# FFT mixing and a gated feed-forward layer on one Trainium2 core: the first batch with one spectrum tile per unit, filters copied across partitions, rotated inverse tables and units by halves of d

## The chip, the core and the metric

The kernel runs on one core of a Trainium2 chip. The core has a matrix engine (TensorE, PE), a vector engine (VectorE, DVE), a scalar engine (ScalarE, ACT), a general engine (GpSimd, POOL) and a queue engine (SyncE, SP). They run side by side, each in its own program order, and wait for each other by semaphores. Sixteen DMA engines move data between the chip's memory and the core's on-chip memory of 128 partitions; SP's DMAs (hardware queue q1) and POOL's (software queue q0) share them. PE writes to PSUM, which DVE and ACT can read and POOL can't. The metric is the device time of one execution in microseconds (us); lower is better.

## The reference

Two stages follow each other; only these lines matter:

```python
def _attn_ref(x, filt_r, filt_i):          # x: 8 x 3008 x 256, filters: 1505 x 256
    X = np.fft.rfft(x, axis=1)
    Y = X * (filt_r + 1j * filt_i)[None, :, :]
    return np.fft.irfft(Y, n=x.shape[1], axis=1).astype(np.float32)

def _moe_ref(x, w_in, w_out, beta):        # x: 24064 x 256, 256 -> 2048 -> 256
    h = x @ w_in
    g = h * (1.0 / (1.0 + np.exp(-beta * h)))
    return (g @ w_out).astype(np.float32)
```

The first stage, run on each of 8 batches along the sequence, filters every column in the frequency domain; the second is a feed-forward layer on all 24,064 rows.

## The kernel before

**The transform as matmuls.** 3008 = 47 x 64. A transform goes in two stages forward (s1 with table t1 over the 47, s2 with tables t2 over the 64, which hold the twiddle factors), a product with the filters, and two stages back (s3 with tables t3, the transposes of t2; s4 with t4, the transpose of t1). Partitions 0 to 63 of a spectrum tile hold real parts, 64 to 127 imaginary parts; the 24 values of k1 (NK) index the tiles. A complex product needs both `real * filt_r - imag * filt_i` and `imag * filt_r + real * filt_i`, so it crosses the two halves of the partitions.

**Main loop.** `NSTEP` = 47 blocks of 512 rows x 16 column blocks of the hidden layer. Step s does two matmuls with w_in (L722, `hps`), one Silu on ACT (L731, `gT`), then whatever the plan puts at this step, then, two steps late, four matmuls with w_out (L742, `acc`). `plan` and `at(step, ...)` are a timetable written out by hand: the transforms of batches 1 to 7 (s1 L557, s2 L573 with the products L587 to L592, s3 L602, s4 L631) are spread over the steps of the batch before. Between s1 and s2, and between s3 and s4, data goes through scratch memory (`d1`, `d2`): stores and loads are SP DMAs, whose queue is in program order. POOL adds the two halves of a product (`yh`, L592), loads x (`load_x`, L332 and L333, a cast from float32 to bf16 in the DMA) and scales w_out by 1/beta (`scale_wout`, L345).

**The setup, batch 0.** Its transform can't hide under anything and runs before the loop, in an order written out by hand. It generates the tables from iotas with Sin on ACT (`t2_part`: two more column sets with another sign, `dup`: copies that put the column blocks side by side in `tw_sb`), loads batch 0 (`x0`, eight DMAs on POOL's queue) and the filters (`load_filters`, L94: half on SP, half on POOL; `seen`, a tiny DMA on SP, holds SP's back until the third quarter of x0 has landed). `s1_0` is stage 1, `a0_turn` transposes its result. Then come six units (8 values of k1 x 128 columns of d): `s2_0` twice per unit, once with the ordinary columns of t2 and once with the halves swapped, each followed by one product on DVE with `ff_sb`, which holds filt_r in partitions 0 to 63 and filt_i in 64 to 127 (L407, L405); `s3_0` sums both products with two sets of inverse tables, `t3c`, made by `t3_part` (transposes, evacuated on ACT). `z_turn` and `s4_0` are the last stage and write y, which the main loop reads; every y write must be there before its first step. Between them stand `s1_early`, the first eight of sixteen stage-1 matmuls of batch 1, and `turn_t4`, which makes t4 (transpose, ACT copy, a POOL multiply of its first rows).

The loop's plan for batch 1 has the other eight stage-1 units in its first six steps, `turn_t3` (L614: t3 from t2, at steps 6, 9, 12), the loads of a2 at step 8 (L565), s2 from step 15, s3 five steps later; at step 4, `copy_fr` (L537, L538: POOL copies filt_r from `ff_sb` to both halves of `fr_sb`, which the products of the loop need, six copies); `load_wout` and `scale_wout` for the third and fourth quarter of w_out at steps 2 and 3. x of batch 2 is loaded at steps 10, 13, 16 and 19.

Evacuations of PSUM go through `evac` (L115 on ACT, L117 and L119 on DVE), so many operations share these lines and are told apart by tile names. `spsum` (three buffers of two banks) and `tpsum` (two) rotate.

Of the kernel before, what the change touches and what calls it, by code (L numbers as in the profile page):

```python
# [10 lines left out]
P = 128  # L11
# [10 lines left out]
N1 = 47  # L22
# [14 lines left out]
def kernel(  # L37
# [40 lines left out]
    ff_sb = consts.tile([P, NK, D], F32, name="ff_sb", tag="ff_sb")  # L78
    fr_sb = consts.tile([P, NK, D], F32, name="fr_sb", tag="fr_sb")
    KH = 8  # L80
    NH = NK // KH

    def load_filters(g):
        k0 = g * KH
        for filt, p0, eng in (
            (filt_i, M, nc.gpsimd),
            (filt_r, 0, nc.sync),
            (filt_r, 0, nc.gpsimd),
            (filt_i, M, nc.sync),
        ):  # L90
            lo = eng is nc.sync
            q0, off, sg = (p0, k0, 1) if lo else (p0 + H, N1 - k0, -1)
            src = AP(filt.tensor, filt.offset + off * D, [[N1 * D, H], [sg * D, KH], [1, D]])
            eng.dma_start(ff_sb[q0 : q0 + H, k0 : k0 + KH, :], src)  # L94
# [3 lines left out]
    tw_sb = consts.tile([P, NK, 5 * M], BF16, name="tw_sb", tag="tw_sb")  # L98
    t2 = tw_sb[:, :, M : 3 * M]
# [21 lines left out]
    E2 = P // 2  # L121
    DG = 8
# [32 lines left out]
    ip = sp.tile([P, 1], I32, name="ip", tag="ip")  # L155

    r_sr = ExitStack()
    sr = rpool("setup_a", r_sr, bufs=1)
    t3c = sr.tile([P, 2, NK, P], BF16, name="t3c", tag="t3c")
# [5 lines left out]
    MQ = M // 4  # L165
# [5 lines left out]
    kk = sq.tile([P, NK, 2, 2], I32, name="kk", tag="kk")  # L171
    c4 = sq.tile([P, NK, 2, 2], I32, name="c4", tag="c4")
    qq = sq.tile([P, NK, 2, 2], I32, name="qq", tag="qq")

    def load_x0(mq):
        ms_ = slice(mq * MQ, (mq + 1) * MQ)
        nc.gpsimd.dma_start(x0[:32, ms_, :], xv0[:32, ms_, :])
        nc.gpsimd.dma_start(x0[32:, ms_, :], xv0[32:, ms_, :])

    load_x0(0)  # L180
# [3 lines left out]
    load_x0(1)  # L184
    iota(vi[:, :, :H], [[1, NK], [N1, H]])
    load_x0(2)
    iota(vi[:, :, H:], [[1, NK], [-N1, H]], base=N1 * (M - 1))
    load_x0(3)
    iota(kk[:], [[1, NK], [0, 2], [0, 2]])
    iota(c4[:], [[0, NK], [1, 2], [0, 2]], base=1)  # L190
    iota(qq[:], [[0, NK], [0, 2], [1, 2]])
# [4 lines left out]
    nc.sync.dma_start(seen[:], x0[:1, 2 * MQ, :2])  # L196
    for g in range(NH):
        load_filters(g)

    pn = small("pn")  # L200
    nc.vector.tensor_scalar_mul(pn[:], ip[:], TURN / N1)
    nc.vector.tensor_scalar_mul(cc[:], cc[:], TURN / 4)
    kcf, ccf = (t[:].rearrange("p a b -> p (a b)") for t in (kc, cc))
    nc.vector.scalar_tensor_tensor(kcf, kcf, pn[:], ccf, ALU.mult, ALU.add)
    fold(kcf)
    nc.scalar.activation(t1d[:], kcf[:N1], ACT.Sin, scale=TWO_PI / TURN)

    m_i = small("m_i", I32)
    c_i = small("c_i", I32)
    ms = small("ms")  # L210
    nc.vector.tensor_scalar(m_i[:], ip[:], M - 1, None, ALU.bitwise_and)
    nc.vector.tensor_scalar(c_i[:], ip[:], 6, None, ALU.logical_shift_right)
    nc.vector.tensor_scalar_mul(ms[:], m_i[:], TURN / S)
    offs = []
    for quarters in (1, 2, 4):
        off = small(f"off{quarters}")
        nc.vector.tensor_scalar(
            off[:], c_i[:], -TURN / 4, quarters * TURN / 4, ALU.mult, ALU.add
        )
        offs.append(off)  # L220

    def t2_part(c2, hi):
        off = offs[c2 * (1 + hi)]
        t = sq.tile([P, NK, H], I32, name="u", tag=f"u{hi}")
        nc.vector.tensor_scalar(  # L225
            t[:], vi[:, :, hi * H : (hi + 1) * H], ms[:], off[:], ALU.mult, ALU.add
        )
        fold(t[:])
        col = c2 * M + hi * H
        nc.scalar.activation(t2[:, :, col : col + H], t[:], ACT.Sin, scale=TWO_PI / TURN)  # L230
# [4 lines left out]
    def s1_0(g, on_act):  # L235
# [11 lines left out]
        evac(aTv[:, g], src, on_act)  # L247
# [10 lines left out]
    def t3_part(c, g, on_act=True):  # L258
        tp = turn8()
        ks = slice(g * KH, (g + 1) * KH)  # L260
        for e in range(KH):
            nc.tensor.transpose(
                tp[:, e, :], tw_sb[:, g * KH + e, 2 * c * M : (2 * c + 2) * M], ident[:]
            )
        evac(t3c[:, c, ks, :], tp[:], on_act)

    def dup(dst, src):
        nc.vector.tensor_copy(
            tw_sb[:, :, dst * M : (dst + 1) * M], tw_sb[:, :, src * M : (src + 1) * M]
        )  # L270

    t2_part(0, 0)
    t2_part(0, 1)
    s1_0(0, False)
    s1_0(1, True)
    t2_part(1, 0)
    s1_0(2, False)
    s1_0(3, True)
    t2_part(1, 1)
    s1_0(4, False)  # L280
    s1_0(5, True)
    nc.vector.memset(t2[:, 0, M : P : M - 1], 0.0)
    dup(4, 1)
    s1_0(6, False)
    s1_0(7, True)
    dup(0, 1)
    dup(3, 2)
    n1s = small("n1s")
    q_p = small("q_p")
    n1_i = small("n1_i", I32)  # L290
    q_i = small("q_i", I32)
    nc.vector.tensor_scalar(n1_i[:], ip[:], 1, None, ALU.logical_shift_right)
    nc.vector.tensor_scalar(q_i[:], ip[:], 1, None, ALU.bitwise_and)
    nc.vector.tensor_scalar_mul(n1s[:], n1_i[:], TURN / N1)
    nc.vector.tensor_copy(q_p[:], q_i[:])
    nc.vector.tensor_scalar(sgn[:], c_i[:], -2.0, 1.0, ALU.mult, ALU.add)

    a0_turn(0, 0, False)
    a0_turn(0, 1, True)
    kkf, c4f, qqf = (t[:].rearrange("p a b c -> p (a b c)") for t in (kk, c4, qq))  # L300
    sn = sq.tile([P, KP], F32, name="sn", tag="sn")
    nc.vector.tensor_scalar_mul(c4f, c4f, TURN / 4)
    nc.vector.scalar_tensor_tensor(kkf, kkf, n1s[:], c4f, ALU.mult, ALU.add)
    fold(kkf)
    nc.scalar.activation(sn[:], kkf, ACT.Sin, scale=TWO_PI / TURN)
    nc.vector.scalar_tensor_tensor(
        t1[:], qqf[:NP], q_p[:NP], sn[:NP], ALU.is_equal, ALU.mult
    )
# [83 lines left out]
    def s2_0(n, swapped):  # L392
        kg, e = units[n]
        ds = slice(e * P, (e + 1) * P)
        ks = slice(kg * KH, (kg + 1) * KH)
        ps = bank2([P, KH, P])
        col = 3 * M if swapped else M
        for kk_ in range(KH):
            k1 = kg * KH + kk_
            nc.tensor.matmul(  # L400
                ps[:, kk_, :], lhsT=tw_sb[:, k1, col : col + P], rhs=a0[:, k1, ds], start=True, stop=True
            )
        r_t = p0pool.tile([P, KH, P], BF16, name="pq_t", tag=f"pq{int(swapped)}")
        if swapped:
            nc.vector.tensor_tensor(r_t[:], ps[:], ff_sb[:, ks, ds], ALU.mult)  # L405
        else:
            nc.vector.scalar_tensor_tensor(  # L407
                r_t[:], ps[:], sgn[:], ff_sb[:, ks, ds], ALU.mult, ALU.mult
            )
        pq[n, swapped] = r_t  # L410

    def s3_0(n):
        kg, e = units[n]
        ps = bank2([P, KH, P])
        for c in range(2):
            src = pq.pop((n, c == 1))
            for kk_ in range(KH):
# [3 lines left out]
                    rhs=t3c[:, c, kg * KH + kk_, :],  # L421
# [3 lines left out]
                )  # L425
        dst = zT[e][:, :WZ].rearrange("p (j k) -> p j k", k=KP)
        kq = P // J
        evac(
# [358 lines left out]
```

## Time and profile before

| what | value |
|---|---|
| median of 10 runs | 802.34 us (801.92 to 806.18) |
| profiled execution, its own time | 802.15 us |
| its span, first to last instruction | 800.4 us |
| mean granted TensorE clock | 0.994 |
| PE busy in the span | 767.0 us (96%) |
| first hps matmuls of the main loop | 47.96 and 49.14 us |
| DMA busy share, 10 to 40 us | 1.00 to 1.07 |
| last DVE copy ends, last issue, landing | 796.21, 796.24, 2.9 us later |

The span is shorter than the execution's time by 1.75 us that lie around it. A row of a timeline reads: start, duration (us), engine, line, operation, output<-inputs, shape, count, and in brackets the engine's idle time before it and what ended it. A row of a group reads: line, engine, operation, tiles, shapes, count, then busy us and mean ns, then idle time before and what ended it. Matmuls are pipelined and their durations are modelled, so PE's throughput is read from the distances between starts.

### The profile page before, as it was taken

How to read it: one execution, taken by the hardware profiler on the slowest of the kernel's cores; microseconds unless marked ns; L12 is line 12 of the kernel's file. 1: busy time of each engine (PE TensorE's matmuls, PEld its weight loads, DVE VectorE, ACT ScalarE, POOL GpSimd, SP SyncE). 2: the span in 40 equal slices, each digit the busy share in tenths (PEclk: the TensorE clock that was granted, in tenths of full speed). 3: DMA queues.
4: the chain of work that ended last, by engine and by line, in shares of the span. 5: the costliest groups of instructions: out<-in, count | busy, mean ns of one | idle time of the engine just before them, and what ended most of it. 6: DMA issues, size and time to landing. Idle time of an engine off the chain costs nothing.

```text
span 800.4 us, 15444 instructions
## 1 busy us (share of the span) xinstructions
PE 767.0 (96%) x6109; PEld 551.7 (69%) x6201; DVE 449.7 (56%) x696; ACT 554.6 (69%) x809; POOL 169.7 (21%) x186
## 2 busy tenths in 40 slices
PE   4886999999999999999999999999999999999997
PEld 4864666766677666776668766786667766676664
DVE  7863775486556665577655766556754666330101
ACT  4773777767667766666667676677766777777775
POOL 7229331132201321023211222011210132000000
PEclk9998999999999999999999999999999999999999
DMA  9956428532662319413393134913255211500101
GB/s 160 234 157 148 103 70 219 145 89 90 155 193 71 89 47 229 145 47 86 83 254 84 54 100 117 249 35 96 64 144 147 71 49 48 152 27 27 54 28 52
DMA packets 84187, 88.29 MB, mean 110 GB/s; under 512 B 5968, under 2 KB 75088, under 8 KB 83736
## 3 DMA queue, kind: packets, MB, share of 16 engines
q1 hardware_dynamic: 79460, 72.37, 30.2%
q0 software_dynamic: 4656, 14.95, 11.1%
q8 instruction: 48, 0.79, 0.4%
q14 instruction: 23, 0.19, 0.1%
HBM read 54.01 MB, written 46.66 MB: 126 GB/s over the span
## 4 chain that ended last, share of the span: by engine, by line
PE 91%; POOL 2%; ACT 2%; DVE 1%; issue 1%; DMA 1%; DVEq 0%; SPq 0%; POOLq 0%; ACTq 0%
PE acc L742 41%; PE hps L722 37%; PE ps L557 3%; PE ps L631 3%; PE ps L602 3%; PE ps L573 2%; DMA ws<-in_moe_w_out_dram 1%; POOL fr_sb L537 1%; PE sps L418 1%; POOL fr_sb L538 0%; ACT t3c L115 0%; PE tps L367 0%; DVE u L225 0%; PE sps L400 0%; POOL wout_sb L345 0%
## 5 line engine op out<-in xcount | busy, mean ns | idle before, releaser
L731 ACT ACTIVATE gT<-hps,beta_sb 128x512 bf16<-128x512 f32 x752 | 516.1, 687 | 222.9 <-PE hps L722 199.6
L742 PE MATMUL acc<-wout_sb,gT 128*128 128x256 bf16 x3008 | 454.3, 273 | 3.6 <-POOL wout_sb L345 0.7
L722 PE MATMUL hps<-y,win_sb 128*128 128x512 bf16 (+7 forms) x1636 | 429.0, 350 | 1.1 <-ACT y L115 1.0
L742 PEld LDWEIGHTS <-gT 128*128 128x128 bf16 x3008 | 287.9, 98 | 126.2 <-issue 3.1
L592 POOL TENSOR_TENSOR yh<-a_t,b_t 128x512 bf16<-128x512 f32 x84 | 106.3, 1265 | 415.5 <-DVE b_t L591 408.6
L722 PEld LDWEIGHTS <-win_sb 128*128 128x128 bf16 x1728 | 165.1, 98 | 25.1 <-DVE y L119 0.8
L753 DVE COPY ost<-acc 128x512 f32<-128x512 f32 x94 | 60.5, 685 | 138.1 <-PE acc L742 138.1
L587 DVE TENSOR_TENSOR a_t<-ps,fr_sb 128x512 f32<-128x512 f32 x84 | 58.1, 692 | 75.9 <-PE ps L573 72.6
L117 DVE CAST a<-ps 96x512 bf16<-96x512 f32 x102 | 69.4, 685 | 47.6 <-PE ps L557 47.0
L119 DVE TENSOR_SCALAR y<-ps 128x376 bf16<-128x376 f32 x104 | 56.0, 548 | 59.4 <-PE ps L631 59.1
L588 DVE SCALAR_TENSOR_TENSOR b_t<-ps,ff_sb 64x512 f32<-64x512 f32 x84 | 58.2, 693 | 1.1
L591 DVE TENSOR_TENSOR b_t<-ps,ff_sb 64x512 f32<-64x512 f32 x84 | 57.4, 684 | 1.1
L117 DVE CAST z<-ps 128x512 bf16<-128x512 f32 x78 | 53.4, 685 | 8.2 <-PE ps L602 7.1
L631 PEld LDWEIGHTS <-zz 96*128 96x128 bf16 x448 | 29.8, 98 | 22.9
L557 PE MATMUL ps<-xg,t 94*96 94x512 bf16 x104 | 39.3, 381 | 0.6
L602 PE MATMUL ps<-yh,t 128*128 128x256 bf16 x168 | 32.3, 274 | 7.2 <-POOL yh L592 6.7
L631 PE MATMUL ps<-t,zz 96*128 96x94 bf16 x448 | 34.7, 205 | 0.7
L602 PEld LDWEIGHTS <-t 128*128 128x128 bf16 x168 | 16.3, 98 | 24.5 <-issue 6.9
L573 PE MATMUL ps<-a,tw_sb 128*128 128x256 bf16 x168 | 32.3, 274 | 0.4
L332 POOL DMA_DIRECT2D xg<-in_x_dram x28 | 15.1, 539 | 65.4 <-PE ps L557 59.3
L573 PEld LDWEIGHTS <-tw_sb 128*128 128x128 bf16 x168 | 16.2, 98 | 16.8 <-issue 0.6
L557 PEld LDWEIGHTS <-t 94*96 94x96 bf16 x104 | 12.8, 123 | 9.8 <-issue 0.3
(94 smaller groups left out, 213.1 us busy)
## 6 DMA issues: line engine op xcount, KB each, us to landing
out_dram<-ost SPq DMA_DIRECT2D x47, 512.0 KB, 3.0
d<-a SPq DMA_DIRECT2D x28, 384.0 KB, 5.0
a<-d SPq DMA_DIRECT2D x28, 384.0 KB, 5.3
d<-z SPq DMA_DIRECT2D x28, 384.0 KB, 3.7
zz<-d SPq DMA_DIRECT2D x28, 384.0 KB, 6.8
xg<-in_x_dram POOLq DMA_DIRECT2D x28, 320.0 KB, 6.0
ws<-in_moe_w_out_dram SPq DMA_DIRECT2D x4, 512.0 KB, 7.2
xg<-in_x_dram POOLq DMA_DIRECT2D x28, 56.0 KB, 5.8
```

Source lines behind the costliest of these rows:

```text
L117: nc.vector.tensor_copy(dst, src)
L557: nc.tensor.matmul(ps[:KP], lhsT=t1[:], rhs=xg[b, g][:, jj : jj + 2, :], start=True, stop=True)
L573: nc.tensor.matmul(ps[:, e, :], lhsT=t2[:, k0 + e, :], rhs=st["a2", b, g][:, kk + e, :], start=True, stop=True,)
L587: nc.vector.tensor_tensor(a_t[:], ps[:], fr_sb[:, ks, :], ALU.mult)
L588: nc.vector.scalar_tensor_tensor(b_t[:M], ps[M:], -1.0, ff_sb[M:, ks, :], ALU.mult, ALU.mult)
L592: nc.gpsimd.tensor_tensor(yh[:], a_t[:], b_t[:], ALU.add)
L602: nc.tensor.matmul(ps[:, e, :], lhsT=t3[:, 2 * i + e, :], rhs=yh[:, e, :], start=True, stop=True)
L631: nc.tensor.matmul(ps[:, e, :NP], lhsT=zz[:, j0 % JG + e, dc * P : (dc + 1) * P], rhs=t4[:], start=True, stop=True,)
L722: nc.tensor.matmul(hps[:, pos - t0 : pos - t0 + ln], lhsT=win_sb[:, dc, fb * P : (fb + 1) * P], rhs=ys[b][:, dc, n0 : n0 + ln], start=(dc ...
L731: nc.scalar.activation(gT[:], hps[:], ACT.Silu, scale=beta_sb[:, fb : fb + 1])
L742: nc.tensor.matmul(acc[tb // 2][:, tb % 2, :], lhsT=gT[:, tb * P : (tb + 1) * P], rhs=wout_sb[:, fb, :], start=(fb == 0 and tb % 2 == 0), ...
L753: nc.vector.tensor_copy(ost[:, 2 * h : 2 * h + 2, :], acc[h][:])
```

## The change

In batch 0, each unit does one `s2_0` and two products from the same PSUM tile, one with `fr_sb`, one with `fi_sb`; each filter must then stand in all 128 partitions. `load_filters` fills one half of each, in three parts cut by d (rows of 128 columns, 512 bytes), SP's parts after `seen`, which waits for the second quarter of x0; `spread` copies the other half on POOL, once per unit. `s3_0` uses `t3` and `t3s`, a rotated copy of t3 (`t3_rotate`, on DVE; the first tile by a transpose of `c10`). t2's second half is a copy of its first, with a sign (`t2_shift`). Units go by halves of d. `spin` adds 26 matmuls whose result isn't used. t3 is made in the setup, so `turn_t3` and `copy_fr` leave the loop. All sixteen stage-1 units of batch 1 stand in the loop's first eight steps, its a2 loads at step 10, its s2 from step 17. Sin's table load is triggered at the very start. The last output block is evacuated by ACT and DVE and stored in two halves.

```diff
-    def load_filters(g):
-        k0 = g * KH
-        for filt, p0, eng in (
-            (filt_i, M, nc.gpsimd), (filt_r, 0, nc.sync),
-            (filt_r, 0, nc.gpsimd), (filt_i, M, nc.sync),
-        ):
...
+    E2 = P
+    def load_filters(eng, k0, k1, d0, d1):
+        lo = eng is nc.sync
+        n = k1 - k0
+        for filt, dst, p0 in ((filt_r, fr_sb, 0), (filt_i, fi_sb, M)):
+            q0, off, sg = (p0, k0, 1) if lo else (p0 + H, N1 - k0, -1)
+            src = AP(filt.tensor, filt.offset + off * D + d0, [[N1 * D, H], [sg * D, n], [1, d1 - d0]])
+            eng.dma_start(dst[q0 : q0 + H, k0:k1, d0:d1], src)
+    parts = ((0, KH, 0, E2), (KH, NK, 0, E2), (0, NK, E2, D))
...
+    nc.scalar.activation(warm[:], warm[:], ACT.Sin)
...
+    load_x0(48, 56)
+    load_x0(56, 64)
+    load_filters(nc.gpsimd, *parts[0])
     make_identity(nc, ident)
...
-    nc.sync.dma_start(seen[:], x0[:1, 2 * MQ, :2])
-    for g in range(NH):
-        load_filters(g)
+    nc.sync.dma_start(seen[:], x0[:1, 16, :2])
+    for part in parts:
+        load_filters(nc.sync, *part)
+    for part in parts[1:]:
+        load_filters(nc.gpsimd, *part)
...
+    def t2_shift(hi):
+        for c in range(2):
+            d0, s0 = (0, M) if c == 0 else (M, 0)
+            dst = t2[d0 : d0 + M, :, M + hi * H : M + (hi + 1) * H]
+            src = t2[s0 : s0 + M, :, hi * H : (hi + 1) * H]
+            if c == hi:
+                nc.vector.tensor_scalar_mul(dst, src, -1.0)
+            else:
+                nc.vector.tensor_copy(dst, src)
...
+    def spin(m, n):
+        ps = tpsum.tile([P, 512], F32, name="tps", tag="tps")
+        for i in range(n):
+            nc.tensor.matmul(
+                ps[:, : 2 * NK], lhsT=x0[:, m + i % 16, :P], rhs=t1d[:], start=True, stop=True
+            )
...
+    def t3_rotate(k0, k1):
+        for c in range(2):
+            nc.vector.tensor_scalar_mul(
+                t3s[:, k0:k1, c * M : (c + 1) * M], t3[:, k0:k1, (1 - c) * M : (2 - c) * M], rot[c][:]
+            )
...
-        if swapped:
-            nc.vector.tensor_tensor(r_t[:], ps[:], ff_sb[:, ks, ds], ALU.mult)
-        else:
-            nc.vector.scalar_tensor_tensor(
-                r_t[:], ps[:], sgn[:], ff_sb[:, ks, ds], ALU.mult, ALU.mult
-            )
+        for c, filt in enumerate((fr_sb, fi_sb)):
+            r_t = p0pool.tile([P, KH, P], BF16, name="pq_t", tag=f"pq{c}")
+            nc.vector.tensor_tensor(r_t[:], ps[:], filt[:, ks, ds], ALU.mult)
...
+    def spread(n):
+        kg, e = units[n]
+        ks = slice(kg * KH, (kg + 1) * KH)
+        ds = slice(e * P, (e + 1) * P)
+        nc.gpsimd.tensor_copy(fr_sb[M:, ks, ds], fr_sb[:M, ks, ds])
+        nc.gpsimd.tensor_copy(fi_sb[:M, ks, ds], fi_sb[M:, ks, ds])
-    units = [(0, 0), (0, 1), (1, 0), (2, 0), (1, 1), (2, 1)]
+    units = [(0, 0), (1, 0), (2, 0), (0, 1), (1, 1), (2, 1)]
...
+    spread(0)
+    spread(1)
     nc.gpsimd.dma_start(win_sb[:], moe_w_in.rearrange("(dc p) f -> p dc f", p=P))
+    spread(2)
+    load_x(1, 0)
+    spread(3)
+    load_x(1, 1)
+    spread(4)
+    spread(5)
+    load_x(1, 2)
+    load_x(1, 3)
...
+    s2_0(0)
+    s2_0(1)
+    t3_rotate(KH, NK)
+    a0_turn(2, 0, True)
+    s3_0(0)
+    s2_0(2)
+    a0_turn(0, 1, True)
+    turn_t4()
+    s3_0(1)
+    s2_0(3)
+    a0_turn(1, 1, False)
+    s3_0(2)
+    s2_0(4)
+    a0_turn(2, 1, False)
+    z_turn(0, 0, True)
+    z_turn(0, 1, True)
+    s3_0(3)
+    s2_0(5)
+    s4_0(0, 0, True)
+    z_turn(0, 2, True)
+    s4_0(0, 1, True)
+    s3_0(4)
+    z_turn(0, 3, True)
+    s4_0(0, 2, True)
...
+    s3_0(5, True)
+    s4_0(0, 3, True)
     z_turn(1, 0, False)
     z_turn(1, 1, True)
+    s4_0(1, 0, False)
     z_turn(1, 2, False)
     z_turn(1, 3, True)
     s4_0(1, 1, True)
...
-            s1_steps(1, range(8, 16), [o + r for r in (0, 1, 1, 2, 3, 4, 4, 5)], False, (10, 14))
-            for g in range(NH):
-                at(o + 6 + 3 * g, turn_t3, g)
+            s1_steps(1, range(16), [o + i // 2 for i in range(16)], False, range(1, 16, 2))
             for g in range(NG):
-                at(o + 8, a2_load, 1, g)
-            s23_steps(1, [o + r for r in (15, 18, 21, 24, 27, 30, 34, 37, 40, 43, 46, 50)], 5, True)
+                at(o + 10, a2_load, 1, g)
+            s23_steps(1, [o + 17 + 3 * i for i in range(NU)], 5, True)
...
-            for g in range(NH):
-                at(4, copy_fr, g)
...
+                rows = out[t0 : t0 + TB, :].rearrange("(c p) d -> p c d", p=P)
+                last = s == NSTEP + LAG - 1
                 for h in range(2):
-                    nc.vector.tensor_copy(ost[:, 2 * h : 2 * h + 2, :], acc[h][:])
-                nc.sync.dma_start(
-                    out[t0 : t0 + TB, :].rearrange("(c p) d -> p c d", p=P), ost[:]
-                )
+                    hs = slice(2 * h, 2 * h + 2)
+                    evac(ost[:, hs, :], acc[h][:], last and h == 0)
+                    if last:
+                        nc.sync.dma_start(rows[:, hs, :], ost[:, hs, :])
+                if not last:
+                    nc.sync.dma_start(rows, ost[:])
```

## The prediction

> **What bounds the kernel now.** I read the page first, then the sums of stages, then the timelines around the one stage that stands out, then the setup.
>
> ```profile
> PE 767.0 (96%) x6109; PEld 551.7 (69%) x6201; DVE 449.7 (56%) x696; ACT 554.6 (69%) x809; POOL 169.7 (21%) x186
> ```
>
> TensorE (PE) is full. From about 160 us on the sums show 99.3 busy in 100 us, and the change touches nothing there before the last output block. What it can win lies where PE is not full: the first 100 us. The sums of four stages (PE, PEld, DVE, ACT, POOL busy, granted clock, DMA share, GB/s):
>
> ```profile
> 50.00:60.00 10.00, 9.92 (x73) 6.60 (x73) 5.24 (x8) 7.23 (x12) 1.23 (x1) 1.00 0.68 200
> 60.00:70.00 10.00, 8.86 (x66) 6.16 (x67) 4.18 (x7) 6.18 (x9) 9.79 (x6) 1.00 0.59 163
> 70.00:80.00 10.00, 3.33 (x17) 1.91 (x16) 2.63 (x4) 1.37 (x2) 9.87 (x12) 0.73 0.63 133
> 80.00:90.00 10.00, 9.89 (x67) 6.90 (x68) 6.90 (x10) 7.01 (x12) 3.99 (x5) 0.93 0.53 114
> ```
>
> In 70 to 80 us PE does a third of its work while POOL is full and the clock falls to 0.73. The timelines of PE and of POOL say why:
>
> ```profile
> 77.64 0.59 PE L602 MATMUL ps<-yh,t 128*128 128x256 bf16 x2 [6.67 <-POOL yh L592]
> 78.02 1.06 PE L742 MATMUL acc<-wout_sb,gT 128*128 128x256 bf16 x4
> 81.67 0.60 PE L742 MATMUL acc<-wout_sb,gT 128*128 128x256 bf16 x4
> ```
>
> ```profile
> 62.58 1.88 POOL L537 COPY fr_sb<-ff_sb 64x2048 f32<-64x2048 f32 x1
> 72.26 1.89 POOL L538 COPY fr_sb<-ff_sb 64x2048 f32<-64x2048 f32 x1
> 76.31 1.27 POOL L592 TENSOR_TENSOR yh<-a_t,b_t 128x512 bf16<-128x512 f32 x1
> ```
>
> Six filter copies (62.58 to 74.15), started late behind the scaling of w_out, hold POOL; the first yh of batch 1 ends at 77.6; PE idles 6.67 us and then runs cold (four acc matmuls: 1.06 for 0.60) until 81.67. The setup ends, and the main loop begins, with the second line here:
>
> ```profile
> 37.55 1.22 DVE L405 TENSOR_TENSOR pq_t<-sps,ff_sb 128x1024 bf16<-128x1024 f32 x1 [0.48 <-PE sps L400]
> ...
> 49.14 0.38 PE L722 MATMUL hps<-y,win_sb 128*128 128x512 bf16 x1 [0.80 <-ACT y L115]
> ```
>
> Rows of the setup that I use as prices (groups of 17 to 49 us), and the two DMA queues at 28 to 30 us:
>
> ```profile
> L405 DVE TENSOR_TENSOR pq_t<-sps,ff_sb 128x1024 bf16<-128x1024 f32 x6 | 7.3, 1218 | 0.5 <-PE sps L400 0.5
> L115 ACT ACTIVATE zT<-sps 128x1024 bf16<-128x1024 f32 x6 | 6.1, 1021 | 2.5 <-PE sps L418 2.5
> L115 ACT ACTIVATE zz<-tps 96x1024 bf16<-96x1024 bf16 x4 | 4.1, 1017 | 2.0 <-PE tps L367 2.0
> L345 POOL TENSOR_TENSOR wout_sb<-ws,rbeta_sb 128x1024 bf16<-128x1024 f32 x2 | 3.7, 1892 | 9.1 <-DVE rbeta_sb L513 9.1
> L115 ACT ACTIVATE y<-sps 128x752 bf16<-128x752 f32 x4 | 3.1, 797 | 0.1
> ```
>
> ```profile
> q0 software_dynamic: 114, 0.33, 83.2%
> q1 hardware_dynamic: 112, 0.11, 20.4%
> ```
>
> Both queues pass the same number of packets (114 and 112): an engine takes one from each in turn, whatever their size.
>
> **The change, part 1: the main loop.** It removes the six copies there (6 x 1.89 on POOL), so yh no longer waits. Gain: 6.67 idle, plus the cold stretch. Between 77.64 and 81.67 PE did 2 ps, 4 acc, 2 hps, 2 ps, 4 acc, 2 hps; warm, by the starts at 81.67, 82.11, 82.54 and 82.76, four acc or two hps take 0.44 and two ps 0.22, so 2.2 for 4.03: 1.83. The three groups of eight transposes for t3 go (58.49 to 58.94: 0.45 each): 1.35. PE waited 0.75 at 60.72 for the third quarter of w_out, whose load stood in SP's queue behind a store of a1 until 52.45, 3.3 us after the loop began. It is now behind the first a1 store, after step 1: issued some 4 us in, landed 6.3 later as before (52.45 to 58.70), scaled in 1.89, so ready at 12.2; wanted at step 10, also about 12.2 (eight steps of 1.31, two of 0.87). I take the 0.75 as gained; the other bound is 0. Added: eight stage-1 matmuls of batch 1 move in from the setup, 0.22 each (two start 0.44 apart at 50.00): 1.74. Their copies out (ACT 0.58, DVE 0.69) fit: a step is then 1.31 on PE and 0.69 + 0.58 on ACT. Batch 1's second stage starts at step 17, some 18.3 us in; its first load waits for the last a1 store (step 7: issue 11.4, landing 3 to 4 later) and landed in 3.3 (61.42 to 64.76): 18.4. I add 0.3 (bounds 0 and 2, with what the stores queue behind). Sum: -6.67 - 1.83 - 0.75 - 1.35 + 1.74 + 0.3 = **-8.6**.
>
> **Part 2: the setup, where it can give this back.** DVE's twelve products stay (1.22 each, the 1.28 form goes); 48 matmuls, 24 transposes and three evacuations of t3c at 1.02 go, the rotations (four, 64-column pieces) come. None of that sets the end, since the products now need all 128 partitions of both filters, and POOL makes the other half: 12 copies of 64x1024. POOL's order is spread 0, spread 1, w_in, spread 2, x, spread 3, x, spread 4 and 5, x, x, then t4. And PE's order puts the first s4_0, which reads t4, ahead of the turns and of s3_0(4): t4 is the new gate.
>
> When does spread 1 start? x0 lands at 13.95 as before (last issue 7.36, 6.6 to landing). POOL's filter loads (1.57 MB) follow on q0 at the 235 to 250 GB/s that the DMA shows at 14 to 24 us: done at about 20.4. SP's 1.57 MB now goes in 512-byte rows, one per turn against q0's 4 KB, so it stands nearly still until then (q0 has 24 filter packets per engine and some 4 of x0 left: 28 of SP's 192 rows), and then runs like the loads of a from d, same size and row (3104 packets at 86.3% of 16 engines in 61.4 to 68 us: 0.029 each): the last 4 rows of part 0 and 64 of part 1, 2.0 us, and the landing. The half of the real filter lands about 0.9 before the other's 22.9: spread 1 starts at about 22.2. Then POOL does ten copies, eight issues of x (0.54), one of w_in (0.78), t4 (0.48). No row has a 64x1024 copy. Bounds: half of 1.89, 0.95; with the fixed share that 1.27 and 1.89 of the 128x512 and 128x1024 products imply, 1.27; I take 1.05, nearer the same operation. 10.5 + 4.3 + 0.8 + 0.5 + 0.3 for semaphores: t4 at 38.6. DVE's last product, fed by spread 5, ends at about 38 and is not later.
>
> After t4 ACT has six y (0.80), four zz (1.02), one zT (1.02) and half a zT (0.55): 10.5. PE leads it by 0.7, and has idled some 5 us by then; after 6.67 idle it ran at half rate for 4 us, so I add 1.2 for a cold start. Main loop at 51.0, against 49.14: **+1.9**. Early bound: t4 no gate, ACT busy from the third zT on (about 33.4, then 13.5): 46.7, -2.4. Late bound: copies at 1.27 (+2.2) and filters 2 late: 55.2, +6.1. Sin's table load moved to the front, the negated t2 copies and the 26 spin matmuls lie under the wait for x0 (PE waits 1.0 to 1.2 before each quarter): nothing; were x0 early, 1.2.
>
> The Trainium skill, DMA: Bandwidth & Descriptors, section Queues, rings and completion order, has an engine drain a packet of some 9 to 17 descriptors before it switches; the equal counts of 1 KB and 4 KB packets above say one row a turn for SP. By the rule the SP rows would land along with POOL's, and spread 1 would start some 2 us sooner. Against the change speaks SBUF — State Buffer, section SBUF: two separate sides: DVE in a two-port mode and GpSimd lock each other out for a whole instruction, so rotations could each wait for a copy. The copies at 62 to 74 us, beside DVE work from PSUM, all took 1.88 to 1.89; by the rule DVE would lose some 2 us, still under t4.
>
> **Part 3: the end.** The last block's two copies (794.92 to 796.21 on DVE) run on ACT and DVE side by side and go out in halves: the last issue moves from 796.24 to about 795.95, with half the bytes. Gain 0.3 to 1.15: **-0.65**.
>
> **Sum.** -8.6 + 1.9 - 0.65 = -7.35 on the profiled execution's 802.15 (span 800.4 and 1.75 around it, kept): 794.8. The median of the runs, 802.34, is 0.2 above that execution, so the two can stand for each other.
>
> **Rivals.** (a) t4 does not gate, ACT does: 802.15 - 2.4 - 9.25 = 790.5. For it: x0's gaps on q0 may let SP's small rows sprint. Against: POOL's ten copies and nine issues cannot shrink. (b) A stall stays at batch 1's second stage: the four loads from d wait for every a1 store on SP behind two 512 KB loads of w_out; 2 us of PE wait and as much again if the clock falls: 794.8 + 4 = 799. Against: those stores start ten steps before. (c) Slower: the filter rows. If a 512-byte row on POOL's queue takes as long as a 1 KB row did, q0 ends 6.4 later, and spread 1 to 5, t4 and the loop with it; with copies at 1.27: 794.8 + 6.4 + 2.2 = 803.4. It decides from a loop start of 49.14 + 9.25 = 58.4, spread 1 at 29.6. For it: this queue was never seen with such rows. Against: on q1 a 512-byte row took 0.029, a 1 KB row 0.058 (20.4% of 32 us over 112). (d) That the copies merely move, gain and loss equal: needs the same 58.4.
>
> **How the numbers follow.** Forecast 791.5 to 798: 0.62. (a) 0.13. (b) 0.10. (c) and (d) 0.15, of which 0.05 within 0.2% (1.6 us, about what a measurement of this kernel can tell from no change) and 0.10 slower. Of (b) 0.01 is no change. Faster 0.84, same 0.06, slower 0.10. Range 790 to 799.5: it holds (a), most of (b), and the late bound of the setup.
>
> **What would show it.** Right: no PE wait over 1 us between 60 and 80, granted clock 1.00 there; POOL full from 22 to 38; PE waiting for t4; main loop at 50 to 52; a last output some 0.6 shorter. Wrong: first s4_0 released by ACT (then a), L566 waiting for a DMA (b), DVE products waiting for filter DMAs beyond 25 us (c).

## The result, and the profile after

The changed kernel takes 799.43 us (median of 10 runs, 798.03 to 801.28) against 802.58 for the kernel before in the same comparison (35 runs): ratio 0.9958, interval 0.9949 to 0.9968. It is faster by 3.15 us, where the forecast was 7.5. Its profiled execution took 801.28 (span 799.3); the sums below are made against that execution, and its setup was one of the long ones, as shown further on.

The page's first part for the changed kernel, then the sums of four stages (PE, PEld, DVE, ACT, POOL busy, granted clock, DMA share, GB/s):

```profile
PE 766.5 (96%) x6040; PEld 550.7 (69%) x6132; DVE 442.8 (55%) x694; ACT 555.6 (70%) x813; POOL 170.5 (21%) x191
```

```profile
50.00:60.00 10.00, 9.18 (x52) 5.33 (x51) 4.59 (x7) 8.28 (x15) 0.00 (x0) 1.00 0.54 159
60.00:70.00 10.00, 8.38 (x58) 5.50 (x58) 1.28 (x2) 7.14 (x11) 4.91 (x4) 1.00 0.72 185
70.00:80.00 10.00, 5.65 (x40) 3.72 (x39) 4.86 (x8) 4.04 (x6) 2.29 (x3) 1.00 0.63 163
80.00:90.00 10.00, 9.89 (x73) 7.14 (x74) 8.15 (x12) 7.28 (x13) 5.91 (x8) 1.00 0.87 158
```

Between 70 and 80 us PE's work rose from 3.33 to 5.65 and the clock from 0.73 to 1.00: the stall behind the filter copies is gone, and so is the cold stretch after it. But PE is still not full there. PE's timeline, the lines with an idle time (in brackets, with what ended it):

```profile
50.61 0.74 PE L704 MATMUL hps<-y,win_sb 128*128 128x512 bf16 x2 [0.53 <-DVE y L116]
57.51 0.38 PE L550 MATMUL ps<-xg,t 94*96 94x512 bf16 x1 [0.23 <-ACT a L112]
61.85 0.38 PE L550 MATMUL ps<-xg,t 94*96 94x512 bf16 x1 [1.57 <-ACT a L112]
73.23 0.39 PE L566 MATMUL ps<-a,t 128*128 128x256 bf16 x2 [2.53 <-DMA a<-d]
76.53 0.38 PE L724 MATMUL acc<-wout_sb,gT 128*128 128x256 bf16 x2 [1.82 <-DVE ost L114]
93.57 0.38 PE L724 MATMUL acc<-wout_sb,gT 128*128 128x256 bf16 x2 [0.81 <-DVE ost L114]
```

Five waits of the loop (the lines from 57.51 on), 6.96 us, none of which the kernel before had. Its own, apart from the 6.67 and 0.75 of the prediction, was one of 0.37 at an output copy. The chain of waits through this stage (start, length, what; pieces left out) links the first four:

```profile
55.80 5.31 DMA d<-a
...
61.21 0.59 ACT a L112
...
62.88 2.99 DMA d<-a
...
65.96 7.23 DMA a<-d
...
75.07 0.68 DVE b_t L584
...
75.79 0.70 DVE ost L114
```

The second a1 store is issued at 55.80 and lands 5.31 later; only then may ACT write into its buffer again (61.21), so the last store goes out at 62.88, the a2 loads at 65.96; the first of these needs 7.23 to land. When it has, DVE's three products of the first second-stage unit (the last at 75.07) stand ahead of an output block's copies (75.79).

The loop starts at 50.61 (forecast 51.0). In the setup, POOL's and PE's timelines:

```profile
21.80 1.04 POOL L460 COPY fr_sb<-fr_sb 64x1024 f32<-64x1024 f32 x1 [1.49 <-DMA fr_sb<-in_filt_r_dram]
...
37.94 0.48 POOL L484 TENSOR_SCALAR t<-t 4x94 bf16<-4x94 bf16 x1
```

```profile
33.02 0.61 PE L423 MATMUL sps<-a,t 128*128 128x128 bf16 x8 [2.24 <-DVE a L114]
...
36.73 1.06 PE L437 MATMUL sps<-t,pq_t 128*128 128x128 bf16 x8
```

Spread 1 starts at 21.80 (forecast 22.2), a 64x1024 copy takes 1.03 to 1.04 (1.05), t4 ends at 38.42 (38.6). The second pair shows something not foreseen: PE waits 2.24 us for the copy of a turn, and then eight matmuls take 1.06 instead of 0.61; the granted clock is 0.50 from 34.1 to 40.9, from about 1 us after that wait has ended.

The end, on ACT, DVE and SP's queue:

```profile
794.64 0.60 ACT L112 ACTIVATE ost<-acc 128x512 f32<-128x512 f32 x1 [0.48 <-PE acc L724]
794.86 0.69 DVE L114 COPY ost<-acc 128x512 f32<-128x512 f32 x1 [12.17 <-PE acc L724]
795.26 0.89 SPq L740 DMA_DIRECT2D out_dram<-ost x2
```

### The profile page after: what moved, and what is told of

It is laid out like the page before. It is cut to its first block, busy times and chain, and to the rows that moved or that the text cites. A ratio compares the mean times of both kernels' runs of the same rounds, so it can differ in the third digit from the quotient of the medians.

```text
span 799.3 us, 15328 instructions
## 1 busy us (share of the span) xinstructions
PE 766.5 (96%) x6040; PEld 550.7 (69%) x6132; DVE 442.8 (55%) x694; ACT 555.6 (70%) x813; POOL 170.5 (21%) x191
## 4 chain that ended last, share of the span: by engine, by line
PE 89%; DMA 5%; ACT 1%; POOL 1%; DVE 1%; issue 1%; SPq 0%; POOLq 0%; ACTq 0%; DVEq 0%
PE acc L724 41%; PE hps L704 37%; PE ps L550 3%; PE ps L617 3%; PE ps L595 3%; PE ps L566 2%; DMA fi_sb<-in_filt_i_dram 2%; DMA d<-a 1%; DMA a<-d 1%; DMA x<-in_x_dram 1%; ACT gT L713 0%; POOL fi_sb L461 0%; ACT a L112 0%; SPq L90 0%; DVE ost L114 0%
## 5 line engine op out<-in xcount | busy, mean ns | idle before, releaser
L116 DVE TENSOR_SCALAR y<-ps 128x376 bf16<-128x376 f32 x104 | 56.0, 548 | 59.0 <-PE ps L617 58.8
L581 DVE SCALAR_TENSOR_TENSOR b_t<-ps,fi_sb 64x512 f32<-64x512 f32 x84 | 58.2, 693 | 1.1
L584 DVE TENSOR_TENSOR b_t<-ps,fi_sb 64x512 f32<-64x512 f32 x84 | 57.4, 684 | 1.1
L550 PE MATMUL ps<-xg,t 94*96 94x512 bf16 x112 | 41.8, 381 | 2.4 <-ACT a L112 1.8
L566 PE MATMUL ps<-a,t 128*128 128x256 bf16 x168 | 32.1, 273 | 2.8 <-DMA a<-d 2.5
L566 PEld LDWEIGHTS <-t 128*128 128x128 bf16 x168 | 16.1, 98 | 19.1 <-DMA a<-d 2.8
L595 PEld LDWEIGHTS <-t 128*128 128x128 bf16 x168 | 16.2, 98 | 17.7
L550 PEld LDWEIGHTS <-t 94*96 94x96 bf16 x112 | 13.8, 123 | 10.5 <-issue 0.3
```

The source lines that it names most:

```text
L550: nc.tensor.matmul(ps[:KP], lhsT=t1[:], rhs=xg[b, g][:, jj : jj + 2, :], start=True, stop=True)
L566: nc.tensor.matmul(ps[:, e, :], lhsT=t2[:, k0 + e, :], rhs=st["a2", b, g][:, kk + e, :], start=True, stop=True,)
L581: nc.vector.scalar_tensor_tensor(b_t[:M], ps[M:], -1.0, fi_sb[M:, ks, :], ALU.mult, ALU.mult)
L584: nc.vector.tensor_tensor(b_t[M:], ps[:M], fi_sb[M:, ks, :], ALU.mult)
L595: nc.tensor.matmul(ps[:, e, :], lhsT=t3[:, 2 * i + e, :], rhs=yh[:, e, :], start=True, stop=True)
```

## The experiments

Twelve kernels, timed in three groups of four beside the kernel before (802.04, 803.17 and 802.48 in them; below `after` the table keeps the order of the groups). Kernels of different groups are better compared by their ratios than by their medians. "Loop" is the time from the first `hps` matmul of the loop to the end of the span, so that setup and loop can be read apart; for the kernel before and those made from it the start is the second `hps` matmul, as in the forecast (49.14).

```
kernel           median (range)            ratio [95%]              loop from  loop length
after            799.43 (798.03-801.28)    0.9958 [0.9949, 0.9968]  50.61      748.7
b_copies_setup   794.29 (793.16-794.94)    0.9899 [0.9884, 0.9915]  50.39      742.1
a_a1x4           797.01 (796.35-797.89)    0.9937 [0.9924, 0.9949]  48.72      745.7
a_x2late         798.01 (797.16-799.52)    0.9950 [0.9937, 0.9962]  49.44      745.9
a_both           796.83 (796.64-797.00)    0.9933 [0.9920, 0.9945]  50.33      744.3
a_steps          796.14 (794.39-796.37)    0.9911 [0.9897, 0.9926]  49.50      742.8
a_t4early        792.97 (792.86-796.44)    0.9893 [0.9874, 0.9911]  48.18      742.6
a_wearly         799.99 (799.53-800.23)    0.9965 [0.9952, 0.9977]  49.21      748.3
b_copies_end     795.61 (792.85-797.25)    0.9911 [0.9893, 0.9928]  48.97      744.1
a_wx             796.65 (796.05-799.09)    0.9929 [0.9917, 0.9942]  50.88      744.4
a_best           792.94 (791.57-794.30)    0.9880 [0.9864, 0.9896]  49.41      741.2
a_turn_act       790.89 (790.62-791.61)    0.9855 [0.9842, 0.9867]  47.38      741.2
b_best           792.35 (791.67-792.73)    0.9871 [0.9858, 0.9883]  49.08      741.3
```

The kernel before had a loop of 751.2.

### What the old stall was worth: b_copies_setup

The kernel before, with its six filter copies emitted in the setup instead of at step 4 of the loop.

```diff
-            for g in range(NH):
-                at(4, copy_fr, g)
...
+    for g in range(NH):
+        copy_fr(g)
     nc.vector.reciprocal(rbeta_sb[:], beta_sb[:])
```

> The kernel before, with the six filter copies moved out of the loop into the setup, where POOL is idle from 33 to 42 us; nothing else changed. Theory 1 (the stall at 71 to 82 us cost what the prediction took for it, 6.67 idle and 1.83 cold, and the change gave it back elsewhere): 8 us faster, about 794, ratio 0.990, no PE wait over 1 us after the loop starts. Rival (the stall hides other waits, so taking it away is worth much less): 2 to 4 us faster, 798 to 800, with a new PE wait at yh, a2 or ost between 65 and 85 us.

Measured 794.29: some 8 us from one edit, more than the whole change gained. Its sums of two stages and its one PE wait at a second stage:

```profile
60.00:70.00 10.00, 9.34 (x74) 6.38 (x73) 4.05 (x6) 6.32 (x10) 5.89 (x7) 1.00 0.64 154
70.00:80.00 10.00, 9.95 (x72) 6.95 (x72) 8.96 (x14) 7.14 (x11) 6.55 (x8) 1.00 0.95 229
```

```profile
66.78 0.39 PE L575 MATMUL ps<-a,tw_sb 128*128 128x256 bf16 x2 [0.48 <-DMA a<-d]
```

PE is full where it stood, at full clock, and the loop is 9.1 shorter: 6.67 + 1.83 + 0.75 + 0.37 less the 0.48 above is 9.1. So the gain side of the forecast was right, and the copies were never the obstacle: POOL had room for them before the loop (which began 1.25 later than in the kernel before here, and 0.06 sooner in b_best, with the same copies). The 0.75 need not be the copies': the wait for w_out is back in b_best (0.77). What the changed kernel did not get was lost elsewhere.

### Where it was lost: a_a1x4, a_x2late, a_both

a1 is the tile that holds results of stage 1 until they are stored to `d1`, a2 the one into which they are loaded back for the second stage. On the changed kernel: four a1 buffers instead of two; x of batch 2 emitted twelve steps later; both.

```diff
-    apool = ctx.enter_context(tc.tile_pool(name="apool", bufs=2))
+    apool = ctx.enter_context(tc.tile_pool(name="apool", bufs=4))
```

```diff
-                    at(o + 14 + 3 * g, load_x, 2, g)
+                    at(o + 26 + 3 * g, load_x, 2, g)
```

> The changed kernel with four a1 buffers in place of two, so that no evacuation of stage 1 of batch 1 waits for a store to land. Theory 1 (two buffers, and stores queued behind w_out loads on SP): the PE waits of 0.23 and 1.57 near 57 and 60 us go, the last a1 store is issued 2 us sooner, and the a2 wait of 2.53 shrinks with it: 2 to 4 us faster than the changed kernel, 795.5 to 797.5. Rival (the loads of a2 are slow for their own reason, x of batch 2 beside them): 1.8 sooner there, but the a2 wait grows by as much: within 0.5 us of 799.4.

> The changed kernel with the loads of x of batch 2 at steps 26, 29, 32, 35 in place of 14, 17, 20, 23; a1 stays at two buffers. Theory 1 (the first x load holds the DMA engines, so that the a2 loads land 7.2 us after issue in place of 3.3): a2 lands near 69.5, the PE waits of 2.53 (a2) and 1.82 (output copies behind late products) go, 3.5 to 4.5 us faster than the changed kernel, about 795.5. Rival (a2 is late because its issue is late): at most 1 us faster.

> Both edits, four a1 buffers and x of batch 2 at steps 26 to 35. Theory 1: all four PE waits between 57 and 77 us go, 0.23 + 1.57 + 2.53 + 1.82 = 6.2 us faster than the changed kernel, 793 to 794, as the prediction had it. Rival (waits move on to yh or to the next loads): 795 or more.

PE's lines in a_a1x4, in a_x2late and (two) in a_both:

```profile
68.25 0.38 PE L566 MATMUL ps<-a,t 128*128 128x256 bf16 x2 [1.55 <-DMA a<-d]
```

```profile
60.33 0.38 PE L550 MATMUL ps<-xg,t 94*96 94x512 bf16 x1 [1.07 <-ACT a L112]
```

```profile
71.81 0.38 PE L724 MATMUL acc<-wout_sb,gT 128*128 128x256 bf16 x2 [1.89 <-DVE ost L114]
...
88.85 0.38 PE L724 MATMUL acc<-wout_sb,gT 128*128 128x256 bf16 x2 [0.81 <-DVE ost L114]
```

With four buffers the stage-1 waits (0.23, 1.57) are gone, and PE still waits 1.55 for a2; 797.01 is within what was expected. With x late the first a2 load lands 3.0 after its issue (64.44 to 67.45) instead of 7.2, and PE no longer waits for it; the stage-1 wait stays (1.07). With both, 1.89 and 0.81 are left, the two in front of output copies, which I had expected to go with the lateness of a2. So a_x2late (798.01) and a_both (796.83) both missed their expectations of about 795.5 and of 793 to 794. These two waits do not depend on a2. DVE's timeline in a_both:

```profile
68.94 0.69 DVE L580 TENSOR_TENSOR a_t<-ps,fr_sb 128x512 f32<-128x512 f32 x1 [8.50 <-PE ps L566]
69.64 0.69 DVE L581 SCALAR_TENSOR_TENSOR b_t<-ps,fi_sb 64x512 f32<-64x512 f32 x1
70.35 0.68 DVE L584 TENSOR_TENSOR b_t<-ps,fi_sb 64x512 f32<-64x512 f32 x1
71.06 1.29 DVE L114 COPY ost<-acc 128x512 f32<-128x512 f32 x2
```

DVE has been idle for 8.50 us, and then gets a unit's three products (2.1 us) and an output block's copies in the same step, in this order: a unit is emitted before the output block of its step, and the first one sits at step 17, which ends a block. PE's next accumulation needs the copied buffer.

### The output copies: a_steps

As a_both, with the second stage of batch 1 moved off steps 17 and 33.

```diff
-            s23_steps(1, [o + 17 + 3 * i for i in range(NU)], 5, True)
+            s23_steps(1, [o + r for r in (18, 21, 24, 27, 30, 34, 37, 40, 43, 46, 48, 50)], 5, True)
```

> The changed kernel with four a1 buffers and x of batch 2 late (as a_both, 796.83), and batch 1's second stage started at step 18 with steps that avoid 17, 33 and 49. Theory: the two waits left in a_both (1.89 at 69.9 and 0.81 at 88.1, PE acc released by DVE ost) come from three products of a unit that stand ahead of the output copies in DVE's queue within the same step, so they go: 796.8 - 2.7 = 794.1 (793.5 to 794.8), no PE wait above 0.5 between 55 and 100 us. Rival: the output copies wait for something else (their accumulator, a DMA of the block before), or the later start makes a wait further down (stage 4's loads): within 0.5 of 796.8.

Both waits are gone, as the theory says. But the unit I had put at step 48 made the same wait at the next block; PE's timeline:

```profile
102.62 0.38 PE L724 MATMUL acc<-wout_sb,gT 128*128 128x256 bf16 x2 [1.48 <-DVE ost L114]
```

So the loop gained 1.5 where 2.7 was expected (744.3 to 742.8), and the rule got a second proof by my own error. The median (796.14) is 1.8 above its profiled run. The mean granted clock of its runs goes down to 0.994; the section on the setup's clock comes back to that.

### Is it the buffers or the neighbours? a_wearly, a_wx

On the changed kernel, still with two a1 buffers: w_out's last two loads issued at the end of the setup; in a_wx also x late, as above.

```diff
     scale_wout(0)
     scale_wout(WG)
+    load_wout(2 * WG)
+    load_wout(3 * WG)
...
-                at(f, load_wout, f * WG)
```

> The changed kernel with only the loads of w_out's third and fourth quarters issued at the end of the setup, ahead of the loop, instead of after its first a1 store. Theory: the stage-1 waits (0.23 and 1.57) and much of the a2 wait (2.53) come from a1 stores that queue behind these two 512 KB loads, not from the number of a1 buffers as such: store 1 lands within 3.5 us of its issue (5.3 now), the 1.57 wait goes, the last a1 store is issued by 61.5 (62.88 now), the a2 loads by 64.6, and the time falls by 1.5 to 3 against the changed kernel (796.4 to 797.9). Rival: the two buffers alone make the wait (a store takes 3 us anyway, and group 2 follows 2.6 us behind group 0's end): a wait of 1 us or more stays at stage 1, gain below 1.

> The changed kernel, still with two a1 buffers, with the loads of w_out's last two quarters ahead of the loop (as a_wearly) and x of batch 2 emitted from step 26 (as a_x2late), so that nothing large runs beside the a1 stores and the a2 loads. Theory: a store takes 3.0 us alone and 5.3 beside any large load (w_out in the changed kernel, x in a_wearly), and only the long landing makes two a1 buffers too few: stores 0 and 1 land within 3.5 us, the stage-1 wait falls to 0.5 or less, the first a2 lands 3 us after its issue, and only the output-copy waits (1.82 and 0.81) stay: as a_both, 796 to 797.3. Rival: two buffers are too few even so: a stage-1 wait of 1 us or more, 798 or above.

a_wearly missed: no gain over the changed kernel, and a longer stage-1 wait. POOL's line and two of PE's say why:

```profile
51.62 0.65 POOL L356 DMA_DIRECT2D xg<-in_x_dram  x1 [0.92 <-PE ps L552]
```

```profile
58.29 0.38 PE L552 MATMUL ps<-xg,t 94*96 94x512 bf16 x1 [2.41 <-ACT a L112]
...
59.04 1.06 PE L705 MATMUL hps<-y,win_sb 128*128 128x512 bf16 x2
```

In the changed kernel POOL waits for w_out and scales it until 64.4, and the x loads of batch 2, next in its queue, wait with it. With w_out early POOL was free, and the x load went out at 51.62, in the loop's second step, though it is emitted at step 14, and just ahead of the first a1 store (52.28), which then took 5.26 to land. The wait for a2 is gone, but after the 2.41 the granted clock is 0.50 for 3.4 us (58.8 to 62.2; two hps take 1.06 for 0.59), so that the loop is only 0.4 shorter. With x held back as well (a_wx), the stores land in 3.0 (53.95 to 56.96, 56.07 to 59.05), two buffers leave a wait of 0.15, a2 lands 3.3 after its issue, and the median is that of a_both. So neither the number of buffers nor one load is the cause by itself: a store takes 3.0 us alone and 4.8 to 5.3 behind a large load, w_out or x, and two buffers cannot bridge the difference. Which of the two is issued first counts: the changed kernel's first store (53.68), issued 0.46 ahead of a w_out load, landed in 3.1.

### The setup's gate and its clock: a_t4early, a_best, a_turn_act

On a_steps: t4 in POOL's order ahead of spreads 4 and 5 and two x loads. Then the steps mended (a_best), then one evacuation moved from DVE to ACT (a_turn_act).

```diff
-    spread(4)
-    spread(5)
-    load_x(1, 2)
-    load_x(1, 3)
...
     turn_t4()
+    spread(4)
+    spread(5)
+    load_x(1, 2)
+    load_x(1, 3)
```

```diff
-(18, 21, 24, 27, 30, 34, 37, 40, 43, 46, 48, 50)
+(18, 20, 22, 24, 27, 30, 34, 37, 40, 43, 46, 50)
```

```diff
-    a0_turn(1, 1, False)
+    a0_turn(1, 1, True)
```

> As a_steps, and POOL's operation on t4 stands before the last two spreads and two x loads (about 32.5 instead of 37.9). Theory of the prediction (t4 gates the end of the setup): the main loop starts 1 to 2 us sooner than in a_steps, and the time is 1 to 2 lower. Rival (in the trace of the changed kernel PE reaches the first matmul that reads t4 only at 39.29, after t4's end at 38.42, held by turns, products and a cold clock): the loop starts within 0.5 us of that of a_steps, and no gain; with the spreads pushed back by 0.5 it may even start 0.5 later.

> All repairs of the changed kernel together: four a1 buffers, x of batch 2 late, t4 early on POOL, and the second stage of batch 1 at steps 18, 20, 22, 24, 27, 30, 34, 37, 40, 43, 46, 50. Theory: a_t4early (792.97) without its one wait left (1.48 at 101 us, output copies behind the products of the unit at step 48): 791.5 (790.8 to 792.2, runs with a cold setup up to 794.5), no PE wait above 0.6 between 50 and 100 us. Rival: the denser first four units make a wait of their own (DVE: three products and a copy per two steps, 2.75 of 2.6 us): within 0.5 of 793.0.

> As a_best, with the copy of the fifth turn of a0 (a0_turn(1, 1)) on ACT instead of DVE, where it stands behind two products; PE waits 2.24 us for it at about 31 us in every trace of the changed setup. Theory: that idle piece is what lets the clock fall in some runs (0.71 at 30 to 35 us, loop start up to 1.9 later): the wait falls under 1.3, the loop starts 0.5 to 1 sooner than in a_best, and the runs lie closer together (within 1.5 us). Rival: PE only waits for the next spread instead, loop start and spread of the runs as in a_best.

t4 then runs at 31.73 instead of 37.96 and the loop starts 1.3 before that of a_steps. Part of this is the clock: the setup of a_steps ran 3.4 us at half clock and that of a_t4early none. The four fastest runs of a_t4early lie within 0.11 us (792.86 to 792.97, clock 0.997 to 0.999), the other two at 795.33 and 796.44 (0.995 and 0.996). At full clock the same setup with t4 late started the loop at 48.72 (a_a1x4, spread 1 at 21.80; here 48.18 and 21.73), so the early t4 is worth some 0.5, where 1 to 2 was expected. What t4 holds back at full clock is seen in a_wearly, whose setup is the changed kernel's but for two loads at its end:

```profile
38.85 0.49 PE L397 MATMUL sps<-t,zz 96*128 96x94 bf16 x8 [0.76 <-POOL t L484]
```

So t4 is a gate, of 0.76 us here and of 0.82, 1.20 and 1.56 in a_a1x4, a_x2late and a_both; in the changed kernel's own trace the cold clock had made PE later still, and t4 was waited for by nobody.

a_best has no PE wait above 0.6 between 50 and 100 us and the loop is 1.4 shorter than in a_t4early, as expected; the median (792.94, where 791.5 was expected) did not follow: the setup of the profiled run was 1.2 later (loop from 49.41) at full clock, and two of the four runs had a clock of 0.996 and 0.997. a_turn_act bears on that. PE's lines for the matmuls that wait for the turn, and the loop's start:

```profile
36.25 0.61 PE L423 MATMUL sps<-a,t 128*128 128x128 bf16 x8 [0.90 <-DVE a L114]
...
47.38 0.59 PE L704 MATMUL hps<-y,win_sb 128*128 128x512 bf16 x2 [0.89 <-ACT y L112]
```

The wait of 2.24 is down to 0.90, and the runs lie within 1.0 us, all at a clock of 0.999 or 1.0. The loop starts 2.0 sooner. Of this 0.9 stands before the moved copy, where x0 and the filters landed earlier (the second half of `s3_0(1)` starts at 28.12, in a_best at 29.06), and 1.1 is the edit's. That the long wait made the cold setups is likely, not shown: two of a_best's four runs had a clock of 1.0 with it. 790.89 is the fastest kernel of the study: the changed kernel with five small repairs, 8.5 us below it.

### The kernel before, repaired: b_copies_end, b_best

b_copies_setup with the change's last output block; then x of batch 2 from step 26 as well.

```diff
-                    at(o + 10 + 3 * g, load_x, 2, g)
+                    at(o + 26 + 3 * g, load_x, 2, g)
```

> The kernel before, with its six filter copies moved into the setup (794.29 when run alone) and the change's last output block (copied by two engines, stored in two halves). Theory: the end is worth the 0.65 that the prediction gave it (bounds 0.3 to 1.15), so 793.6 (793.1 to 794.0), and the last output is issued about 0.5 sooner after the last matmul. Rival: the landing of the last transfer has a fixed length of about 2.4 to 2.9 us whatever its size, and a second issue costs as much as the copy saves: within 0.25 of 794.3.

> The kernel before with three edits: its six filter copies in the setup, the change's last output block, and x of batch 2 from step 26 instead of 10. Theory: the spread of b_copies_end (792.85 to 797.25) came from x of batch 2 landing beside the four a2 loads (its traced run waits 2.00 us for a2, landing 5.3 after the issue); without it 792.6 (792.0 to 793.2) with runs within 1.5 us. Rival: the a2 loads are slow for the w_out loads and a1 stores before them, or the setup makes the spread: a wait of 1 us or more for a2 stays, or the range stays 4 us.

b_copies_end is inconclusive by its median (795.61, runs from 792.85 to 797.25). Its trace prices the end all the same: from the last silu's start to the span's end it takes 5.8 us (787.29 to 793.1) against 6.6 in b_copies_setup (785.89 to 792.5), 0.8 less. The scatter fits the neighbours again; in its profiled run x was issued at 61.12, just ahead of a2 at 61.30, and a2 took 5.2 to land:

```profile
66.59 0.39 PE L575 MATMUL ps<-a,tw_sb 128*128 128x256 bf16 x2 [2.00 <-DMA a<-d]
```

The granted clock is then 0.50 from 67.6 to 71.0. In b_copies_setup the order was the other way round, a2 at 63.24 and x at 63.33: a2 landed in 3.5, and PE waited the 0.48 shown above. With x late (b_best) the wait is gone, and the runs lie within 1.1 us around 792.35, as expected. Three small edits to the kernel before thus give 10 us, within 1.5 of the best version of the rewritten one.

## Why the prediction was right or wrong

**The direction and the main gain: right.** The stall and the cold stretch: b_copies_setup finds 9.1 in the loop, and 6.67 and 1.83 of it are the forecast's terms.

**The step that failed: "I add 0.3 (bounds 0 and 2, with what the stores queue behind)".** It was to cover all that moving stage 1 into the loop does to batch 1's second stage. It measured 6.96 in the profiled run, 6.6 net of the 0.37 before, and is nearly the whole difference between the forecast loop (742.0) and the measured one (748.7). The store time used there, "3 to 4", was that of a store with nothing beside it, and the load time, 3.3, that of a load with nothing beside it; the working named the two w_out loads in the same queue and did not add them. Three further things were not asked at all: how many a1 buffers there are, and so what waits for a store to land (1.8); what POOL issues once it is free of w_out (the x loads, 2.53 at a2); and what else DVE has to do at the step where the new unit stands (2.63). Each is shown by an experiment: a_a1x4 removes the first alone, a_x2late the second alone, and a_steps all of the third on top of these two. The profiled execution is 6.5 above the forecast, the median 4.6; the difference is the setup, below.

**Rival (b)** named the right place and, for the stores, the right queue, with 4 us and a chance of 0.10, and gave 799 for 799.43. Of its price only 2.53 was a wait for a2, and no clock fell; it was nearly right in its sum by the waits that it did not name. "Against: those stores start ten steps before" does not hold: a store that starts early still delays whoever needs its buffer.

**Moved work: right.** Without waits the changed loop is 741.2 long (a_best, a_turn_act), the forecast 742.0 less the 0.3. Against b_best, which still has a w_out wait of 0.77, it is 0.6 longer without one; 1.74 for eight matmuls less 1.35 for the turns made it 0.4.

**The setup: right in size (50.61 for 51.0), by two errors that cancelled; that is luck.** With t4 done at 38.37 and the clock full, the loop started at 48.72 in a_a1x4, which has the same setup: 10.3 after t4, where the forecast had 10.5 + 0.7. The cold start put at 1.2 was 6.8 us at half clock in the profiled run, whose loop starts 1.9 later than a_a1x4's, and was absent in others. Also, DVE's last product was not done by 38: it ran from 38.84 in a_a1x4 and from 40.73 here, and PE waited for it (0.41 and 0.67). In the early bound, 33.4 + 13.5 makes 46.9, not 46.7. Sums of the stage from 36 to 37 us, the changed kernel first, then a_a1x4:

```profile
36.00:37.00 1.00, 1.00 (x11) 1.00 (x11) 0.67 (x2) 0.03 (x1) 1.00 (x3) 0.50 1.09 219
```

```profile
36.00:37.00 1.00, 1.00 (x22) 1.00 (x20) 0.70 (x2) 0.70 (x1) 1.00 (x3) 1.00 1.12 225
```

PE is busy all the time in both and does 11 matmuls in the one, 22 in the other. Both had idled for the same 2.2 us before. The profiled run (801.28) is 1.85 above its kernel's median; of the ten runs the five above 799.5 have a mean clock of 0.994 to 0.996.

**The filter rows: right in time, wrong in mechanism.** I let SP's 512-byte rows pass one per turn of POOL's queue, against a rule of the Trainium skill. The packets of the two queues in the changed kernel (packets, MB, time share) from 14 to 16 us and from 20 to 22 us:

```profile
q1 hardware_dynamic: 635, 0.31, 89.2%
q0 software_dynamic: 44, 0.11, 24.3%
```

```profile
q0 software_dynamic: 118, 0.40, 87.1%
q1 hardware_dynamic: 117, 0.06, 17.1%
```

At 20 to 22 it is one for one, as in the row I read. At 14 to 16, where spread 1 is decided, SP's queue passes 14 rows for each of POOL's packets: SP's parts 0 and 1 had landed by 18.99, and spread 1 waited for POOL's own part (real filter 21.75). The Trainium skill, DMA: Bandwidth & Descriptors, section Queues, rings and completion order, has an engine drain some 9 to 17 descriptors of a queue before it switches; the first stretch agrees with it, the second does not, and no run here shows what tells them apart, nor whether POOL's queue always had packets waiting in the first. Rival (c) needed spread 1 at 29.6 and a loop start of 58.4, rival (d) the same start; they fall with 21.80 and 50.61.

**The lock between DVE and POOL: shown, and nearly free here.** Two rotations of 448 columns beside a POOL copy in the changed kernel, and the same in a_steps, where POOL waited for a filter until 20.32:

```profile
19.04 1.42 DVE L323 TENSOR_SCALAR t3s<-t,rot 128x448 bf16<-128x448 bf16 x2
```

```profile
19.01 0.59 DVE L323 TENSOR_SCALAR t3s<-t,rot 128x448 bf16<-128x448 bf16 x2
```

The 0.83 more is the rest of POOL's copy (19.28 to 20.32), which one rotation waited out. This agrees with the Trainium skill, SBUF — State Buffer, section SBUF: two separate sides, by which one of the two engines is shut out for the other's whole instruction. POOL waits for filters until 21.80 anyway. It is not free everywhere: the later pair of rotations (128x1024) took 1.10 in the changed kernel and 1.73 in a_best, where a copy of POOL's began (27.23) just before it (27.28), and PE waited for it 0.81 in the one and 1.44 in the other.

**The end: right**, 0.8 for 0.65. Rival (a), 790.5, needed t4 to gate nothing. In the profiled run nobody waited for t4, but the setup was slow for its clock, and at full clock t4 does gate (0.76 to 1.56).

## What to carry to other kernels

Work that is moved next to other work has to be priced with all that it touches there: the buffers that its stores hold, every transfer on the same DMA engines in that stretch, and what each engine's queue already has to do in the very step it is put into. A transfer's landing time from a quiet stretch is no price for a busy one. And a load on an in-order engine starts when that engine is free, not at the step that it is written at: whoever frees the engine starts the load.

## What was not expected of the hardware

- A PE wait of some 2 us can be followed by half clock. Of the nine traces of the changed setup with the turn's wait (2.23 or 2.24, in a_both 2.95), three show it (the changed kernel, a_steps, a_wx) and six do not, a_both among them; with the wait at 0.90 none of four runs shows it. In the loop it followed waits of 2.41 (a_wearly) and 2.00 (b_copies_end), not one of 2.53 (the changed kernel). Each time it lasted 3.4 or 6.8 us. What decides between the two, and whether it comes at all, no run here shows. It makes a good part of the spread of the runs, not all: a_both's loop started at 50.33 at full clock, its filters having landed late.
- A 384 KB store to DRAM landed in 3.0 us alone, and in 5.3 behind a 512 KB load on its own queue or a 376 KB load on POOL's; a 384 KB load landed in 3.0 alone and in 5.2 to 7.2 behind x, and in 3.5 when it was issued 0.09 ahead of x.
- Two queues shared the engines 14 to 1 in rows in one stretch and 1 to 1 in another, with the same row sizes on SP's side.
